# Gated MLP behind a gated linear attention: the gating multiply walks its columns in write order

## The chip, the cores and the metric

The kernel runs on one core of one Trainium2 chip. The metric is the device time of one execution in microseconds, the median of several runs. Five engines work side by side and meet through semaphores: TensorE (PE, with its weight loads PEld), VectorE (DVE), ScalarE (ACT), GpSimd (POOL) and SyncE (SP), which issues the transfers. Matmul results land in PSUM, eight banks of 512 float32 values per partition; everything else stays in SBUF.

## The reference, cut to what matters

A gated linear attention with 32 heads of width 48 over 768 tokens, and behind it a two-layer MLP whose activation is `h * cos(h)`:

```python
for t in range(S):
    state = f[:, :, t, :, None] * state + k[t] outer v[t]      # f = sigmoid(f_logit)
    y[:, :, t] = q[t] @ state
x = y as (4*768 tokens, 384)
h = x @ w_in            # 384 -> 2048
g = h * np.cos(h)       # the gating
out = g @ w_out         # 2048 -> 384
```

Inputs and output are float32; the kernel works in bfloat16 between them and accumulates in float32.

## The kernel before, in words

**Attention.** The tokens are taken in 12 pairs of 128-token chunks (`pair(n)`). For each pair the kernel loads f, k, q and v, forms decays on ACT and PE, decayed q and k on POOL, their transposes, the scores `sc` on PE, the masked scores `am` on DVE (L461), the carried state `st` and `sz` on DVE (L497, L503), and the outputs `y` and `yi` on PE. `xe` (DVE or ACT, L197) copies these into `x`, the MLP's input. A pair of chunks holds 256 tokens, of which each partition row loaded two neighbours; so inside a chunk of 128 columns the token order is e-major: column `64*e + n` holds token `2*n + e`.

**MLP.** `moe(m, t0, T)` takes a unit of T = 128 (the first two) or 256 tokens. The 2048 hidden features are computed in steps of 1024 columns of PSUM, which is two banks: step `h{m}.{j}` (PE, L579) is 4 feature blocks of 128 by 256 tokens (or 8 by 128), 12 matmuls of 256 columns (or 24 of 128). Step `co{m}.{j}` (ACT, L584) takes the cosine of these 1024 columns, as a sine with a phase, into the bfloat16 tile `co` in SBUF. Step `g{m}.{j}` (DVE, L561, function `gate`) multiplies `ph` (PSUM, float32) by `co` and writes `g` (SBUF, bfloat16). Steps `o{r}.{s}` (PE, L595) multiply four feature blocks of g with w_out, four matmuls of 384 columns each; `ot` copies the sums out of PSUM and `out` stores them.

**The token order in the gating.** `ph` and `co` have the e-major order of x. `g` is written in plain token order, column `2*n + e`, so that the output rows come out in order. So the multiply is also a permutation of each chunk's 128 columns, done by the access patterns of its three operands. There are 48 such multiplies, each over 128 partitions and 1024 columns.

**Order and buffers.** Every step has its engine and its place in one list written out by hand (`ORDER`). `g7.2:V` means that step g7.2 runs on DVE, and a number or letter behind it chooses engine and buffer; each engine runs its steps in this order. The PSUM tiles are four, of two banks each; an `h` step takes one whole tile (places T0, T2, T4, T6), and a tile is free for the next step when the gating that reads it has ended. Smaller results (scores, sums of `o`) use the same tiles. `co` has four buffers, `g` five.

Of the kernel before, what the change touches and what calls it, by code (L numbers as in the profile page):

```python
# [188 lines left out]
def describe(nc, cpool, ppool, q, k, v, f_logit, moe_w_in, moe_w_out, out):  # L189
# [368 lines left out]
    def gate(gv, ph, co, T):  # L558

        o = gv.ap if T == C else gv.ap.rearrange("p f (g t) -> p (f g) t", t=C)  # L560
        nc.vector.tensor_mul(out=o.rearrange("p b (n e) -> p b e n", e=2),  # L561
                             in0=ph.ap.rearrange("p (b e n) -> p b e n", e=2, n=64),
                             in1=co.ap.rearrange("p (b e n) -> p b e n", e=2, n=64))


    def moe(m, t0, T):
# [4 lines left out]
        for j in range(KF // F):  # L571
            ph, co = Val(p2), Val(coS)
            for s in range(2):
                def first(e, j=j, s=s, ph=ph):
                    xa = xw.ap if T == 2 * C else xw.ap[:, None]
                    for i in range(s * F // 2, (s + 1) * F // 2):
                        f0 = (j * F + i) * 128
                        for kk in range(KM):
                            nc.tensor.matmul(ph.ap[:, i * T:(i + 1) * T].rearrange("p (g t) -> p g t", t=C),  # L579
                                             lhsT=w_in_bf[:, kk, f0:f0 + 128], rhs=xa[:, :, kk, :], start=(i % (F // 2) == 0 and kk == 0),  # L580
                                             stop=((i + 1) % (F // 2) == 0 and kk == KM - 1))
                G.step(f"h{m}.{j}{s}", ("PE",), first, reads=[xw, w_in_v[(j * F + s * F // 2) // 4]],
                       writes=[ph], sums=True)
            G.step(f"co{m}.{j}", ("ACT",), lambda e, ph=ph, co=co: nc.scalar.activation(  # L584
                out=co.ap, in_=ph.ap, func=AF.Sin, bias=halfpi), reads=[ph], writes=[co], table="S")
            gv = gT.part(lambda a, j=j: a[:, j * F:(j + 1) * F, 0:T])
            G.step(f"g{m}.{j}", ("DVE",), lambda e, ph=ph, co=co, gv=gv: gate(gv, ph, co, T),
                   reads=[ph, co], writes=[gv])
# [129 lines left out]
```

## Time and profile before

| | |
|---|---|
| time, median of 3 runs | 183.58 us (183.56 to 183.68) |
| the profiled execution | 183.05 us, span 181.3 us |
| PE busy | 174.0 us, 96% of the span |
| DVE busy | 138.2 us, 76% |
| ACT busy | 130.7 us, 72% |
| POOL busy | 109.2 us, 60% |
| the gating, 48 instructions on DVE | 61.3 us busy, 1311 ns each |
| the cosine, 48 instructions on ACT | 52.7 us busy, 1113 ns each |

Busy times are those of one profiled execution; its time is 1.75 us longer than its span, which runs from the first to the last instruction. A group of instructions is named by source line, engine, operation and operands, with its count, busy time and the mean duration of one; behind a bar stands the idle time of the engine just before them and what ended it. Back-to-back instructions on DVE overlap a little in the records, so a group's busy time is less than count times mean.

### The profile page before, as it was taken

The page shows a single profiled execution, that of the slowest core. Times are in us where ns is not written, and L with a number is a line of the kernel's source. Part 1 is how long each engine was busy: PE and PEld are TensorE (multiplying, and loading weights), DVE is VectorE, ACT ScalarE, POOL GpSimd, SP SyncE. Part 2 cuts the span into 40 slices and gives each one's busy share as a digit, 9 for nine tenths or more (in the row PEclk, how much of TensorE's full clock was granted, in tenths as well). Part 3 has the DMA queues.
Part 4 walks back from the last instruction along what each step waited for, and adds up shares of the span by engine and source line. Part 5 has one row for each costly group of instructions (what it writes and reads, how often), then busy time and mean ns, then how long its engine had stood idle before and what let it go on. Part 6 is the DMA issues. An engine that isn't in the chain of part 4 may idle for free.

```text
span 181.3 us, 5818 instructions
## 1 busy us (share of the span) xinstructions
PE 174.0 (96%) x2464; PEld 124.2 (69%) x2464; DVE 138.2 (76%) x206; ACT 130.7 (72%) x187; POOL 109.2 (60%) x139
## 2 busy tenths in 40 slices
PE   7999788999999999999999999999999999999992
PEld 2555357785677876778657886658788767786661
DVE  5359988898685989897999698689888994466260
ACT  3985988778877999989997899769768452473221
POOL 4229889999969996989755968790799000000000
PEclk9999999999999999999999999999999999999999
DMA  6999999999999945996889999749929400110313
GB/s 141 261 261 263 346 304 318 293 283 281 317 264 241 270 77 128 253 230 133 125 162 317 189 242 253 175 125 244 216 85 197 90 4 0 38 52 4 130 43 130
DMA packets 72282, 33.93 MB, mean 187 GB/s; under 512 B 65344, under 2 KB 70720, under 8 KB 72256
## 3 DMA queue, kind: packets, MB, share of 16 engines
q1 hardware_dynamic: 71584, 33.27, 76.6%
q8 instruction: 19, 0.31, 0.7%
q10 hardware_dynamic: 672, 0.30, 0.6%
q14 instruction: 7, 0.06, 0.1%
HBM read 25.17 MB, written 4.72 MB: 165 GB/s over the span
## 4 chain that ended last, share of the span: by engine, by line
PE 80%; DMA 8%; SPq 5%; DVE 3%; POOL 1%; issue 1%; ACT 1%; POOLq 0%
PE ps L595 35%; PE ps L579 32%; DMA k<-in_k_dram 5%; PE ps L531 5%; SPq L296 3%; PE ps L456 3%; DMA v<-in_v_dram 3%; PE ps L479 2%; DVE g L561 1%; SPq L282 1%; PE ps L435 1%; PE ps L374 1%; DVE am L461 1%; POOL qk L404 1%; POOL k L351 1%
## 5 line engine op out<-in xcount | busy, mean ns | idle before, releaser
L561 DVE TENSOR_TENSOR g<-ps,co 128x1024 bf16<-128x1024 f32 x48 | 61.3, 1311 | 15.8 <-ACT co L584 14.8
L595 PE MATMUL ps<-w_out_bf,g 128*128 128x384 bf16 x384 | 68.9, 326 | 0.0
L579 PE MATMUL ps<-x,w_in_bf 128*128 128x256 bf16 (+1 forms) x624 | 68.2, 264 | 0.6 <-DVE x L197 0.5
L584 ACT ACTIVATE co<-ps,halfpi 128x1024 bf16<-128x1024 f32 x48 | 52.7, 1113 | 20.0 <-PE ps L579 19.8
L579 PEld LDWEIGHTS <-w_in_bf 128*128 128x128 bf16 x624 | 56.3, 98 | 9.3 <-DVE x L197 0.7
L595 PEld LDWEIGHTS <-g 128*128 128x128 bf16 x384 | 36.0, 98 | 21.5 <-issue 0.3
L461 DVE TENSOR_TENSOR am<-ps,pmask 128x1024 bf16<-128x1024 f32 x24 | 28.7, 1218 | 5.0 <-PE ps L456 4.8
L404 POOL TENSOR_TENSOR qk<-k,bi 128x384 bf16<-128x384 f32 x22 | 22.0, 1010 | 5.4 <-ACT bi L391 4.7
L404 POOL TENSOR_TENSOR qk<-q,b 128x384 bf16<-128x384 f32 x21 | 20.9, 1004 | 2.7 <-DVE q L338 2.1
L197 POOL COPY vt<-vb 64x384 bf16<-64x384 bf16 x33 | 16.7, 507 | 1.6
L264 PE MATMUL ps<-zero 128*128 128x512 bf16 x54 | 16.1, 426 | 1.2 <-DVE zero L203 1.2
L503 DVE TENSOR_TENSOR sz<-ps,b 64x192 bf16<-64x192 f32 x40 | 14.1, 353 | 2.5 <-PE ps L479 1.6
L341 POOL TENSOR_TENSOR q<-f,q 128x384 f32<-128x384 f32 x10 | 10.0, 1000 | 8.3 <-DMA q<-in_q_dram 6.1
L363 POOL TENSOR_TENSOR sp<-ls 128x384 bf16<-128x384 f32 x10 | 10.2, 1015 | 7.7 <-ACT ls L333 5.9
L329 ACT ACTIVATE f<-f 128x768 f32<-128x768 f32 (+1 forms) x14 | 10.4, 746 | 4.5 <-DMA f<-in_f_logit_dram 4.4
L351 POOL TENSOR_TENSOR k<-k,f 128x384 f32<-128x384 f32 (+1 forms) x12 | 11.1, 930 | 4.2 <-DMA k<-in_k_dram 4.2
L497 DVE TENSOR_TENSOR ps<-ps,sz 64x192 f32<-64x192 f32 x32 | 11.7, 366 | 1.9 <-PE ps L479 0.8
L197 ACT COPY ot<-ps 128x384 f32<-128x384 f32 (+1 forms) x14 | 6.1, 453 | 8.7 <-PE ps L595 8.7
L197 ACT CAST x<-ps 128x384 bf16<-128x384 f32 x12 | 5.5, 479 | 5.9 <-PE ps L531 5.9
L456 PE MATMUL ps<-qkt 48*64 48x128 bf16 (+1 forms) x304 | 8.7, 219 | 1.0 <-DVE sz L503 0.8
L197 DVE CAST x<-ps 128x384 bf16<-128x384 f32 x12 | 6.4, 552 | 4.0 <-PE ps L531 3.8
L264 PEld LDWEIGHTS <-zero 128*128 128x128 bf16 x54 | 4.9, 105 | 6.1 <-issue 2.2
(64 smaller groups left out, 167.5 us busy)
## 6 DMA issues: line engine op xcount, KB each, us to landing
v<-in_v_dram SPq DMA_DIRECT2D x12, 384.0 KB, 6.0
out_dram<-ot SPq DMA_DIRECT2D x22, 192.0 KB, 2.1
f<-in_f_logit_dram SPq DMA_DIRECT2D x10, 384.0 KB, 6.0
k<-in_k_dram SPq DMA_DIRECT2D x10, 384.0 KB, 6.7
q<-in_q_dram SPq DMA_DIRECT2D x10, 384.0 KB, 6.7
g<-in_moe_w_in_dram SPq DMA_DIRECT2D x4, 768.0 KB, 7.6
g<-in_moe_w_out_dram SPq DMA_DIRECT2D x4, 768.0 KB, 5.8
k<-in_k_dram SPq DMA_DIRECT2D x4, 192.0 KB, 4.5
```

The source lines that it names most:

```text
L197: (nc.scalar.copy if e == "ACT" else eng(e).tensor_copy)(out=o, in_=i)
L264: G.step(f"zf{i}", ("PE",), lambda e, dump=dump: nc.tensor.matmul(dump.ap, lhsT=zero[:, 0:128], rhs=zero, start=True, stop=True), writes=[ ...
L351: eng(e).tensor_mul(out=w.ap[:, :, 0, :], in0=w.ap[:, :, 0, :], in1=t.ap[:, :, 0, :])
L404: G.step(f"{nm}{n}.{u}", ("POOL", "DVE") if cut else ("POOL",), lambda e, u=u, j=j, src=src, dec=dec: eng(e).tensor_mul(out=qkp[u][j].ap[: ...
L456: nc.tensor.matmul(o[t0:t1, r, 2 * a + g, :].rearrange("p (e n) -> p e n", e=2), lhsT=wide[s, t0 // 64, :] if turned else wide[s].rearrang ...
L461: G.step(f"am{n}.{u}", ("DVE",), lambda e, u=u, sc=sc: nc.vector.tensor_mul(out=am[u].ap.rearrange("p r b n -> p (r b) n"), in0=sc.ap.rear ...
L497: nc.vector.tensor_add(out=view()[s], in0=view()[s], in1=S0.ap[s, :, r, :])
L503: eng(e).tensor_mul(out=new.ap[s, :, r, :].rearrange("p (u a) n -> p u a n", u=2), in0=view()[s].rearrange("p (u a) n -> p u a n", u=2), i ...
L561: nc.vector.tensor_mul(out=o.rearrange("p b (n e) -> p b e n", e=2), in0=ph.ap.rearrange("p (b e n) -> p b e n", e=2, n=64), in1=co.ap.rea ...
L579: nc.tensor.matmul(ph.ap[:, i * T:(i + 1) * T].rearrange("p (g t) -> p g t", t=C), lhsT=w_in_bf[:, kk, f0:f0 + 128], rhs=xa[:, :, kk, :], ...
L584: G.step(f"co{m}.{j}", ("ACT",), lambda e, ph=ph, co=co: nc.scalar.activation(out=co.ap, in_=ph.ap, func=AF.Sin, bias=halfpi), reads=[ph], ...
L595: nc.tensor.matmul(po.ap[:, 0:DM], lhsT=gT.ap[:, j, i * C:(i + 1) * C], rhs=w_out_bf[:, j, :], start=(po.first and j == 4 * s), stop=(po.f ...
```

## The change

In `gate` the names in the access patterns change place, from `p b e n` to `p b n e`, on all three operands:

```diff
     def gate(gv, ph, co, T):
         o = gv.ap if T == C else gv.ap.rearrange("p f (g t) -> p (f g) t", t=C)
-        nc.vector.tensor_mul(out=o.rearrange("p b (n e) -> p b e n", e=2),
-                             in0=ph.ap.rearrange("p (b e n) -> p b e n", e=2, n=64),
-                             in1=co.ap.rearrange("p (b e n) -> p b e n", e=2, n=64))
+        nc.vector.tensor_mul(out=o.rearrange("p b (n e) -> p b n e", e=2),
+                             in0=ph.ap.rearrange("p (b e n) -> p b n e", e=2, n=64),
+                             in1=co.ap.rearrange("p (b e n) -> p b n e", e=2, n=64))
```

The same products land in the same places. Before, the instruction walked along its inputs, column 0, 1, 2 and so on, and its writes went in steps of two bfloat16 elements (4 bytes), first the even and then the odd columns of a chunk. After, it walks along its output, column by column, and its reads alternate between the two halves of a chunk: 0, 64, 1, 65, 2, 66 and so on. In `ph` a step of 64 is 256 bytes of PSUM, in `co` it is 128 bytes of SBUF. Instruction count, engines, order, buffers and semaphores are those of before.

## The prediction

> **What bounds the kernel now.** I read the page first: the busy shares, then the chain of work that ended last.
>
> ```profile
> span 181.3 us, 5818 instructions
> PE 174.0 (96%) x2464; PEld 124.2 (69%) x2464; DVE 138.2 (76%) x206; ACT 130.7 (72%) x187; POOL 109.2 (60%) x139
> PE 80%; DMA 8%; SPq 5%; DVE 3%; POOL 1%; issue 1%; ACT 1%; POOLq 0%
> ```
>
> PE sets the time: it holds 80% of the chain, and the rest of it is the start (loads and their issue) and the last copies. DVE stands second with 138.2 of 181.3 us, and holds 3% of the chain. A dearer instruction on DVE therefore costs nothing until it makes PE wait. The waits of PE on DVE, all of them, are these:
>
> ```profile
> PE ps L264 <- DVE zero L203: 1.2, 1, 1.2
> PE ps L435 <- DVE qk L404: 1.0, 2, 0.8
> PE ps L456 <- DVE sz L503: 0.8, 1, 0.8
> PE ps L579 <- DVE x L197: 0.5, 1, 0.5
> PE ps L456 <- DVE qkt L197: 0.2, 1, 0.2
> ```
>
> 3.7 us in all, and none of it behind the gating. So the gating is late for nobody today. How much later it may get is a question of the stretches where it runs in a row. I take the five dense ones, then the whole middle and the end. The columns are the window, its length, and busy time and count by engine; an instruction that reaches over an edge is counted by its share. The second answer is the same for the gating line alone.
>
> ```profile
> 28.10:43.60 15.50, 14.65 (x218) 11.74 (x216) 14.65 (x15) 12.03 (x13) 15.27 (x15) 1.00 1.07 304
> 58.85:68.60 9.75, 9.75 (x119) 7.91 (x117) 9.23 (x8) 9.01 (x9) 8.78 (x11) 1.00 0.78 176
> 79.08:90.60 11.52, 11.52 (x172) 9.04 (x169) 10.42 (x12) 10.76 (x14) 10.43 (x12) 1.00 0.76 147
> 101.78:115.10 13.32, 13.32 (x167) 10.50 (x164) 10.17 (x9) 11.91 (x13) 10.27 (x12) 1.00 1.12 230
> 127.31:147.40 20.09, 20.09 (x287) 15.59 (x288) 17.87 (x19) 13.96 (x18) 11.98 (x16) 1.00 0.59 128
> 28.10:150.00 121.90, 121.05 (x1907) 90.72 (x1906) 105.25 (x141) 99.04 (x131) 92.27 (x111) 1.00 0.87 203
> 150.00:181.30 31.30, 28.01 (x253) 19.68 (x250) 13.90 (x15) 10.58 (x13) 0.00 (x0) 0.99 0.16 58
> ...
> 28.10:43.60 15.50, 10.20 (x8) 1.00 1.07 304
> ...
> 28.10:150.00 121.90, 51.10 (x40) 1.00 0.87 203
> 150.00:181.30 31.30, 10.21 (x8) 0.99 0.16 58
> ```
>
> From 28.10 to 150 us DVE (the third busy number) is at work for 105.25 of 121.90 us and runs 40 of the 48 gatings; in the five dense stretches it is at work for 14.65 + 9.23 + 10.42 + 10.17 + 17.87 = 62.34 of 70.18 us. The share of 76% over the whole span hides this: where the gating runs, DVE has 7.84 us left, and in the whole middle 16.65 us. Behind 150 us more than half of its time is free.
>
> **The change: the price of one gating.** Nothing is added, removed or moved; 48 instructions get other access patterns. Their price comes from three rows of groups on DVE:
>
> ```profile
> L561 DVE TENSOR_TENSOR g<-ps,co 128x1024 bf16<-128x1024 f32 x48 | 61.3, 1311 | 15.8 <-ACT co L584 14.8 <-POOL qk L404 0.6
> L461 DVE TENSOR_TENSOR am<-ps,pmask 128x1024 bf16<-128x1024 f32 x24 | 28.7, 1218 | 5.0 <-PE ps L456 4.8
> L197 DVE COPY ot<-ps 128x384 f32<-128x384 f32 x10 | 5.2, 550 | 0.9 <-PE ps L595 0.8
> ```
>
> The masked scores `am` are the same operation as the gating, from PSUM and SBUF to SBUF, on the same types and the same 1024 columns, but with all three operands read and written in runs of 128 and more. From `am` (1024 columns) and `ot` (384 columns), both out of PSUM, one column costs (1218 - 550) / 640 = 1.044 ns, and an instruction has 1218 - 1069 = 149 ns beside its columns. The gating is 93 ns above `am`. I read these 93 ns as the price of its stepped write, since `am` lacks nothing else that is plain to see; it is 0.09 ns a column, for one stream whose step is as small as it can be.
>
> No row shows DVE reading in steps of more than one element, so the new price is bounded from both sides. Below: the write becomes a plain run and the reads cost nothing, 1218 ns as `am`, 93 ns less than today. [...] I take 1931 ns, two thirds of the way up (1218 + 1069 x 2/3), 620 ns more than today. [...]
>
> [...]
>
> **From the price to the time.** 40 gatings in the middle add 40 x 0.62 = 24.8 us to DVE. At most, all of DVE's 16.65 idle us there take it up, and 8.2 us are left over; at least, only the idle time inside the dense stretches does, and 17.0 us are left. PE has no idle time there (121.05 of 121.90 us), so what makes PE wait is paid in full, and where PE waits, ACT's cosines and DVE's own next inputs come later too. To choose between the two I follow the fourth stretch:
>
> ```profile
> 100.56 9.33 PE L579 MATMUL ps<-x,w_in_bf 128*128 128x256 bf16 x84
> 103.87 5.03 DVE L561 TENSOR_TENSOR g<-ps,co 128x1024 bf16<-128x1024 f32 x4 [0.77 <-ACT co L584]
> 109.73 4.71 PE L595 MATMUL ps<-w_out_bf,g 128*128 128x384 bf16 x28
> 109.77 3.82 DVE L561 TENSOR_TENSOR g<-ps,co 128x1024 bf16<-128x1024 f32 x3 [0.87 <-ACT co L584]
> 115.10 1.23 DVE L461 TENSOR_TENSOR am<-ps,pmask 128x1024 bf16<-128x1024 f32 x1 [1.51 <-PE ps L456]
> ```
>
> 84 matmuls are seven steps h of 9.33 / 7 = 1.33 us. The last of them, h7.0, begins at about 108.56 and writes the tile that g8.2 leaves. g8.2 is the third of the row of four, which starts every (5.03 - 1.31) / 3 = 1.24 us, so it ends at 103.87 + 2.48 + 1.31 = 107.66: 0.9 us of cover. Three dearer gatings (the one before the row falls into the 0.77 us of idle time) put it 3 x 0.62 = 1.86 us later: PE stands 0.96 us. The next PE step, o11.3, takes the tile of g7.2, the fourth, which ends at 103.87 + 5.03 = 108.90 and then 4 x 0.62 = 2.48 later at 111.38; PE would come at 109.89 + 0.96 = 110.85: 0.53 us more, 1.5 us in all. DVE then runs its next three at 1.24 + 0.62 = 1.86 us, is done at about 111.38 + 3 x 1.86 = 116.96, and begins `am` at once, 1.86 us later than the 115.10 of today. The rule "added time less the idle time in the stretch" gives 8 x 0.62 - (13.32 - 10.17) = 1.8 us. So here the 17.0 rule holds, and most of it is seen by PE on the spot through the tiles that come free late. In the first stretch the rule is too strict, as an attention part with idle time follows it. I take 14.5 us, nearer to the upper end.
>
> Behind 150 us eight gatings come singly or by twos and threes with idle time ahead of them. The last one counts:
>
> ```profile
> 172.00 6.01 PE L595 MATMUL ps<-w_out_bf,g 128*128 128x384 bf16 x36
> 173.34 1.31 DVE L561 TENSOR_TENSOR g<-ps,co 128x1024 bf16<-128x1024 f32 x1 [3.25 <-ACT co L584]
> ```
>
> It is g12.0 and ends at 174.65. The 36 matmuls are nine steps o of 0.67 us, and the written order puts five of them ahead of o22.0, the first that reads it: 172.00 + 5 x 0.67 = 175.3. The cover is 0.7 us, and the added 0.62 us costs nothing there (0.3 us at the upper price).
>
> Sum, against the profiled execution's own 183.05 us (span 181.3 and 1.75 around it): 183.05 + 14.5 = 197.6 us. The median of the runs, 183.58, is 0.53 above that execution, so the forecast is **198 us**. With the price's upper end the middle adds 39.0 us, of which 22.4 to 31.2 remain: up to 215 us. A price of 1600 ns adds 11.6 us, of which 3.8 remain by the stricter rule: 187 us. The forecast's own range is 187 to 215.
>
> **The rivals.** *The reads cost nothing.* Each read stream alternates between two places, and each of the two advances one element at a time; if the engine keeps both neighbourhoods at hand, it pays nothing for that, and the write is plain as for `am`. The gating then takes 1218 ns, 93 less. For it: nothing in the profile, which has no such read; against it: the 93 ns themselves, a price for a milder walk. As PE waits nowhere for the gating, the gain is confined to the place where the chain runs through it. Of the chain in order of time these are the pieces:
>
> ```profile
> 28.10 1.33 DVE g L561
> ...
> 30.64 1.23 DVE g L561
> ```
>
> Two gatings, 2 x 0.093 = 0.2 us: 183.4 us, not slower. This case decides if the gating's row stays below some 1310 ns. [...]
>
> *The hops add.* PSUM and SBUF may each ask a cycle of its own, three in all: 149 + 3 x 1069 = 3356 ns, 2.05 us more; the middle adds 82 us, of which 65 to 74 remain, about 250 us. Anything above 2287 ns belongs here, from 215 us on. [...]
>
> *The cover is enough.* With a price between 1310 and 1600 ns the 40 gatings add less than 12 us, and the idle time of the middle takes up most of it: 183.6 to 187 us. For it: PE waits nowhere for the gating today. Against it: the dense stretches leave DVE 7.84 us for 40 gatings, 0.2 us each.
>
> That the multiply is carried out in the old order all the same, as the two orders give the same result, would leave 1311 ns and 183.6 us; I know no row that speaks for it.
>
> **How the numbers follow.** The measurement can tell about 0.2%, 0.37 us, from no change. Chances: the forecast (1600 to 2287 ns) 0.65, free reads 0.15, the hops add 0.10, the cover 0.08, the old order 0.02. Slower takes the forecast, the adding hops and 0.06 of the cover: 0.81. Free reads split into 0.07 faster and 0.08 the same, as 0.2 us lies inside what can be told; with 0.02 of the cover and 0.02 of the old order the same has 0.12. The range of 8 in 10 takes in the free reads at 183.2 and ends at the forecast's upper end of 215.
>
> **What would show it.** The gating's group should read near 1930 ns x48 (about 93 us) and DVE near 168 us. PE should lose its gapless stretches at L579 and L595, with new waits on "DVE g L561", and DVE should go over 90% between 28 us and the end of the attention; ACT's cosine should keep 1113 ns. If the gating reads near 1930 ns but the time is under 192 us, the step from DVE to PE was wrong; if the gating reads below 1600 or above 2287 ns, the price was.

## The result, and the profile after

The changed kernel takes 182.91 us (median of 21 runs, 182.29 to 183.44) against 183.41 us of the kernel before (21 runs): the ratio is 0.9972, with a 95% interval of 0.9959 to 0.9985. Measured once more beside other kernels it was 0.9983 (0.9964 to 1.0003). The first interval excludes a ratio of 1, the second just contains it. So it is a little faster, by 0.3 to 0.5 us, where 198 us was forecast. The median lies 0.3 us below the range's lower end of 183.2.

The page of the kernel after, busy shares and chain:

```profile
span 180.9 us, 5814 instructions
PE 172.6 (95%) x2460; PEld 123.9 (69%) x2464; DVE 134.6 (74%) x206; ACT 130.7 (72%) x187; POOL 109.2 (60%) x139
PE 81%; DMA 7%; ACT 3%; DVE 3%; SPq 2%; issue 1%; ACTq 0%
```

DVE has 3.6 us less to do; the chain is PE's as before. The groups of the gating and of the masked scores show why:

```profile
L561 DVE TENSOR_TENSOR g<-ps,co 128x1024 bf16<-128x1024 f32 x48 | 57.4, 1220 | 18.0 <-ACT co L584 16.7
L461 DVE TENSOR_TENSOR am<-ps,pmask 128x1024 bf16<-128x1024 f32 x24 | 28.7, 1218 | 5.2 <-PE ps L456 4.9
```

The gating costs 1220 ns, as the masked scores do: the surcharge of 93 ns is gone and the alternating reads cost nothing that can be told (2 ns). Of the 3.9 us that the gating's busy time loses (61.3 to 57.4), 2.2 us turn up as idle time ahead of it (15.8 to 18.0). The window of the whole middle says the same: DVE at 101.91 instead of 105.25 us, PE at 121.23 instead of 121.05 of 121.90 us.

```profile
28.10:150.00 121.90, 121.23 (x1909) 91.04 (x1904) 101.91 (x141) 99.01 (x131) 91.60 (x110) 1.00 0.85 201
```

What reached the end can be followed in the order of time. First the kernel before, from the first gating to the second pause for attention; then the kernel after:

```profile
28.10 1.33 DVE L561 TENSOR_TENSOR g<-ps,co 128x1024 bf16<-128x1024 f32 x1 [0.65 <-POOL qk L404]
...
37.93 5.14 DVE L561 TENSOR_TENSOR g<-ps,co 128x1024 bf16<-128x1024 f32 x4
39.75 0.82 PE L579 MATMUL ps<-x,w_in_bf 128*128 128x256 bf16 x6
40.57 0.45 PEld L595 LDWEIGHTS <-g 128*128 128x128 bf16 x4 [0.28 <-issue]
40.60 0.81 PE L595 MATMUL ps<-w_out_bf,g 128*128 128x384 bf16 x4
...
44.07 1.47 PE L595 MATMUL ps<-w_out_bf,g 128*128 128x384 bf16 x8
```

```profile
27.95 1.23 DVE L561 TENSOR_TENSOR g<-ps,co 128x1024 bf16<-128x1024 f32 x1 [0.65 <-issue]
...
37.64 3.48 DVE L561 TENSOR_TENSOR g<-ps,co 128x1024 bf16<-128x1024 f32 x3
39.45 0.82 PE L579 MATMUL ps<-x,w_in_bf 128*128 128x256 bf16 x6
40.11 0.45 PEld L595 LDWEIGHTS <-g 128*128 128x128 bf16 x4
40.14 0.81 PE L595 MATMUL ps<-w_out_bf,g 128*128 128x384 bf16 x4
...
43.61 1.47 PE L595 MATMUL ps<-w_out_bf,g 128*128 128x384 bf16 x8
```

Counted from the first gating, PE's h step at 39.75 comes 11.65 us later before and 11.50 after (-0.15), and the first o step 12.50 and 12.19 (-0.31). The second difference is a wait that the table of waits does not list. This first o step is o2.0, and in the written order it takes the PSUM tile T0, which g0.1, the second gating of the row at 37.93, has to read first. Before, g0.1 starts at 39.15 and ends at 40.45. PE's weight loads for o2.0 begin 0.12 us later, at 40.57, after 0.28 us of standing idle, although the six matmuls ahead, which start 0.109 us apart, 0.66 us in all, would by an estimate from that have let PE go on at 40.41. After, g0.1 ends at 39.99 and the loads begin at 40.11, again 0.12 us later; PE is ready just then (39.45 + 0.66). The eight-matmul o step then stands at 15.97 and 15.66 us. From there to the last row of 36 o matmuls it is 172.00 - 44.07 = 127.93 before and 171.58 - 43.61 = 127.97 after: no further gain is seen in the following 128 us. A gain of a few tenths would not be seen here, since the changed kernel, profiled a second time, took 172.00 - 43.61 = 128.39 us for this stretch.

### The profile page after: what moved, and what is told of

It is laid out like the page before. It is cut to its first block, busy times and chain, and to the rows that moved or that the text cites. A ratio compares the mean times of both kernels' runs of the same rounds, so it can differ in the third digit from the quotient of the medians.

```text
span 180.9 us, 5814 instructions
## 1 busy us (share of the span) xinstructions
PE 172.6 (95%) x2460; PEld 123.9 (69%) x2464; DVE 134.6 (74%) x206; ACT 130.7 (72%) x187; POOL 109.2 (60%) x139
## 4 chain that ended last, share of the span: by engine, by line
PE 81%; DMA 7%; ACT 3%; DVE 3%; SPq 2%; issue 1%; ACTq 0%
PE ps L595 35%; PE ps L579 33%; PE ps L531 5%; DMA f<-in_f_logit_dram 4%; PE ps L456 4%; DMA v<-in_v_dram 3%; SPq L296 2%; PE ps L479 2%; DVE g L561 1%; PE ps L435 1%; PE ps L374 1%; DVE am L461 1%; PE ps L264 1%; ACT f L344 0%; ACT f L329 0%
## 5 line engine op out<-in xcount | busy, mean ns | idle before, releaser
L561 DVE TENSOR_TENSOR g<-ps,co 128x1024 bf16<-128x1024 f32 x48 | 57.4, 1220 | 18.0 <-ACT co L584 16.7
L584 ACT ACTIVATE co<-ps,halfpi 128x1024 bf16<-128x1024 f32 x48 | 52.7, 1113 | 19.8 <-PE ps L579 19.5
L461 DVE TENSOR_TENSOR am<-ps,pmask 128x1024 bf16<-128x1024 f32 x24 | 28.7, 1218 | 5.2 <-PE ps L456 4.9
L264 PE MATMUL ps<-zero 128*128 128x512 bf16 x50 | 14.6, 412 | 1.5 <-DVE zero L203 1.2
```

Source lines behind the costliest of these rows:

```text
L264: G.step(f"zf{i}", ("PE",), lambda e, dump=dump: nc.tensor.matmul(dump.ap, lhsT=zero[:, 0:128], rhs=zero, start=True, stop=True), writes=[ ...
L461: G.step(f"am{n}.{u}", ("DVE",), lambda e, u=u, sc=sc: nc.vector.tensor_mul(out=am[u].ap.rearrange("p r b n -> p (r b) n"), in0=sc.ap.rear ...
L561: nc.vector.tensor_mul(out=o.rearrange("p b (n e) -> p b n e", e=2), in0=ph.ap.rearrange("p (b e n) -> p b n e", e=2, n=64), in1=co.ap.rea ...
```

## The experiments

The first question is where the time came from; the second what a read or a write in steps costs; the third whether the prediction's rule from price to time holds.

**The new order in the first eight gatings alone (early), and in the other 40 alone (late).** The edit, shortened:

```diff
+        if m <= 2:          # early; late: m > 2
             nc.vector.tensor_mul(out=o.rearrange("p b (n e) -> p b n e", e=2), ...)
+        else:
+            nc.vector.tensor_mul(out=o.rearrange("p b (n e) -> p b e n", e=2), ...)
```

Expected of early:

> The new order only in the eight gatings of units 0 to 2 (the first 43 us), the old order in the other 40. Theory: PE waits nowhere for the gating except through the start of its chain, so the whole gain comes from the first gatings and this kernel keeps it: ratio to before near 0.997, eight gatings at 1220 ns, forty at 1311. Rival: each of the 48 gatings gives its share of the gain; then eight of 48 give a ratio near 0.9995, which is the same as before.

Expected of late:

> The new order only in the 40 gatings of units 3 to 12, the old order in the first eight. Theory: PE is covered there, so 40 x 0.09 = 3.6 us less on DVE turn into idle time of DVE and the ratio is 1.000 (0.999 to 1.001). Rival (equal shares): 0.9977.

Measured: early 183.47 against 183.62 us, ratio 0.9989 (0.9978 to 0.9999); late 183.49 us, ratio 0.9999 (0.9989 to 1.0009). Their groups, early first, show that both did what they say:

```profile
L566 DVE TENSOR_TENSOR g<-ps,co 128x1024 bf16<-128x1024 f32 x40 | 51.1, 1309 | 15.0 <-ACT co L589 14.7
L562 DVE TENSOR_TENSOR g<-ps,co 128x1024 bf16<-128x1024 f32 x8 | 9.6, 1217 | 1.0 <-POOL qk L404 0.7 <-ACT co L589 0.3
```

```profile
L562 DVE TENSOR_TENSOR g<-ps,co 128x1024 bf16<-128x1024 f32 x40 | 47.8, 1220 | 17.1 <-ACT co L589 16.3
L566 DVE TENSOR_TENSOR g<-ps,co 128x1024 bf16<-128x1024 f32 x8 | 10.2, 1315 | 0.7 <-issue 0.7
```

Late has 3.3 us less gating and no gain. Its interval rules out equal shares of all 48 gatings, which would have given 0.9977; early's own interval does not rule them out (0.9995). In early's order of time the same o step as above comes 43.55 - 27.90 = 15.65 us behind the first gating, in late's 44.06 - 28.09 = 15.97: the 0.31 us are the first eight gatings'. That is a ratio of 0.9983, inside the intervals of early and of the changed kernel. The 0.997 expected of early was too much. Whether the other 40 add one or two tenths of a microsecond the runs cannot tell.

**The changed kernel again (after2).**

> The changed kernel once more, beside the kernel before and on the same chip as the other three. If 0.3 us of gain from the first eight gatings is all there is, the ratio is 0.998 to 0.9985; if the other 40 add to it, 0.997 or below.

0.9983 (0.9964 to 1.0003), 183.14 against 183.60 us. It fits 0.3 us, but its interval does not exclude the other case, and the two medians lie 0.46 us apart.

**Reads in other walks (read_a).** The 44 gatings of units 2 to 12 in four kinds, each on its own line; s is 2, 8 or 32. This kernel and the next three on reads and writes were run once each, so a price below is that of 8 to 11 instructions in one run:

```diff
+            nc.vector.tensor_mul(out=flat.rearrange("p (s a) -> p s a", s=8),
+                                 in0=ph.ap.rearrange("p (a s) -> p s a", s=8),
+                                 in1=co.ap.rearrange("p (a s) -> p s a", s=8))
```

> The 44 gatings of units 2 to 12 write a plain run and read both inputs in other walks, eleven each: plain; every second column, twice over; every eighth column, eight times over (128 places visited in turn); every 32nd (32 places in turn). The order of g's columns is left wrong by this. Theory A (reads never pay for a step): all four 1218 to 1225 ns. Theory B (the engine keeps only a few neighbourhoods at hand, two in the changed kernel): plain and every second column near 1220, every eighth and every 32nd column dearer, up to 2290 ns. If plain reads and a plain write come out below 1218 ns, something in the changed gating still pays.

The groups: L568 plain, L572 every second column, L576 every eighth, L580 every 32nd.

```profile
L576 DVE TENSOR_TENSOR g<-ps,co 128x1024 bf16<-128x1024 f32 x11 | 21.9, 2004 | 0.9 <-ACT co L603 0.8
L580 DVE TENSOR_TENSOR g<-ps,co 128x1024 bf16<-128x1024 f32 x11 | 20.8, 1898 | 3.6 <-ACT co L603 3.6
...
L572 DVE TENSOR_TENSOR g<-ps,co 128x1024 bf16<-128x1024 f32 x11 | 13.4, 1221 | 3.3 <-ACT co L603 3.0
L568 DVE TENSOR_TENSOR g<-ps,co 128x1024 bf16<-128x1024 f32 x11 | 13.4, 1218 | 4.8 <-ACT co L603 4.7
```

So reads in steps can cost what was forecast, 1.9 to 2.0 us, but not every such read does: theory A falls.

**Which memory, and how many places (read_b).** The same with 512, 256 and 128 columns between places, and steps of 32 on one input alone.

> As the first run on reads, eight or nine gatings each: two places in turn, 512 columns apart (for PSUM in different banks); four places, 256 apart; eight places, 128 apart; 32 places in steps of 32 from PSUM alone with co read plainly; the same from co alone with PSUM read plainly (the order of g's columns is left wrong by this). Theory (a few neighbourhoods are kept at hand): two places 1220 ns whatever their distance; a jump to some 1900 ns at four or at eight places tells how many are kept. For the source: if each memory charges alike and the two overlap, both single ones read near 1900 ns; if only SBUF or only PSUM charges, one reads 1220. Rival (it is the length of the step that costs, not the number of places): two places at 512 dearer than 1220.

L568 is two places, L572 four, L576 eight, L580 steps of 32 from PSUM alone, L584 steps of 32 from SBUF alone.

```profile
L568 DVE TENSOR_TENSOR g<-ps,co x9: 1208/1220/1234, 38.3 to 175.4; 128x1024 bf16<-128x1024 f32 x9
L572 DVE TENSOR_TENSOR g<-ps,co x9: 1917/1932/1951, 42.1 to 169.3; 128x1024 bf16<-128x1024 f32 x9
L576 DVE TENSOR_TENSOR g<-ps,co x8: 1912/1943/1960, 59.2 to 164.3; 128x1024 bf16<-128x1024 f32 x8
L580 DVE TENSOR_TENSOR g<-ps,co x9: 1214/1223/1225, 34.2 to 180.1; 128x1024 bf16<-128x1024 f32 x9
L584 DVE TENSOR_TENSOR g<-ps,co x9: 1870/1891/1925, 35.4 to 172.3; 128x1024 bf16<-128x1024 f32 x9
```

The columns behind the count are minimum, median and maximum in ns. In steps of 32 columns the PSUM read costs nothing that can be told (L580, 128 bytes, 1223 ns); all of the price is the SBUF read's (L584, 64 bytes, 1891 ns). Two places are free at both distances run, 64 columns (1220 ns in the changed kernel) and 512 (1220 ns); four, 256 apart, are not (1932 ns), and three were not run. Steps of 32 are the only walk that was run on each memory alone.

**Two places or near neighbours (read_c).** Walks that tell "two places are kept" from "a neighbour was read just before" (the line of `co` of each; `ph` is read in the same walk, `out` written plainly):

```diff
+  in1=co.ap.rearrange("p (a s) -> p s a", s=4)               # every fourth
+  in1=co.ap.rearrange("p (a s e) -> p e s a", a=2, e=2)      # two places, each by 2
+  in1=co.ap.rearrange("p (a s e) -> p e s a", a=2, e=8)      # two places, each by 8
+  in1=co.ap.rearrange("p (a s r) -> p s a r", a=4, r=2)      # four places, runs of 2
+  in1=co.ap.rearrange("p (a s r) -> p s a r", a=4, r=4)      # four places, runs of 4
```

> [...] Walks: every fourth column (8 bytes of co); two places 512 columns apart, each moving on by 2 columns (4 bytes, so that no 4-byte word is visited twice); the same, each moving on by 8 columns (16 bytes); four places with runs of 2 columns (4 bytes); four places with runs of 4 columns (8 bytes). Theory P (two places are kept at hand): both two-place walks 1220 ns, four places about 1940 with runs of 2 and of 4 alike or less with runs. Theory N (an element is cheap when it lies near one read one or two elements before, whatever the number of places): two places moving on by 2 near 1220, moving on by 8 near 1940 or above, as the 2004 of every eighth column; runs of 4 in four places near 1220.

In that order, L568 to L584:

```profile
L568 DVE TENSOR_TENSOR g<-ps,co x9: 1211/1217/1226, 38.0 to 171.2; 128x1024 bf16<-128x1024 f32 x9
L572 DVE TENSOR_TENSOR g<-ps,co x9: 1215/1229/1240, 41.8 to 165.1; 128x1024 bf16<-128x1024 f32 x9
L576 DVE TENSOR_TENSOR g<-ps,co x8: 2069/2078/2089, 58.8 to 160.7; 128x1024 bf16<-128x1024 f32 x8
L580 DVE TENSOR_TENSOR g<-ps,co x9: 1216/1223/1225, 34.1 to 175.7; 128x1024 bf16<-128x1024 f32 x9
L584 DVE TENSOR_TENSOR g<-ps,co x9: 1206/1217/1225, 35.4 to 167.4; 128x1024 bf16<-128x1024 f32 x9
```

Theory P falls: two places are dear when each moves on by 16 bytes (2078 ns). The three forecasts of theory N came true, and the two other walks fit it: the walks over co that were free are those in which every read had another close to it, next to it in order or with one other read between. For neighbours in order 8 bytes were near enough (every fourth column, 1218 ns) and 16 were not (every eighth, 2004 ns); with one read between 4 bytes were (1229 ns) and 16 were not (2078 ns); distances between these were not run. The changed gating reads 0, 64, 1, 65 of each chunk (1220 ns), so the next read but one is 2 bytes on. That the price of the dear walks is SBUF's was shown for steps of 32 alone (L580 and L584 of read_b, 1223 and 1891 ns); in the others a price of PSUM could hide behind that of SBUF.

**Writes in other walks (write_a).** Both inputs read plainly, `out` in steps:

```diff
+            nc.vector.tensor_mul(out=flat.rearrange("p (a s) -> p s a", s=2),
+                                 in0=ph.ap.rearrange("p (s a) -> p s a", s=2),
+                                 in1=co.ap.rearrange("p (s a) -> p s a", s=2))
```

> The 44 gatings read both inputs plainly and write g in other walks, eight or nine each: two places in turn, 512 apart; every second column (the step of the old gating, over 1024 columns); every eighth; every 32nd; every 128th, eight places (the order of g's columns is left wrong by this). If the 93 ns of the old gating are the price of its stepped write, every second column reads near 1310 ns, and longer steps the same or more. Rival (the 93 ns came from something else in the old pattern, such as its 16 runs of 64): every second column near 1220 ns.

L568 two places, L572 every second column, L576 every eighth, L580 every 32nd, L584 every 128th:

```profile
L568 DVE TENSOR_TENSOR g<-ps,co x9: 4664/4714/4923, 44.2 to 280.3; 128x1024 bf16<-128x1024 f32 x9
L572 DVE TENSOR_TENSOR g<-ps,co x9: 1290/1311/1528, 52.4 to 268.6; 128x1024 bf16<-128x1024 f32 x9
L576 DVE TENSOR_TENSOR g<-ps,co x8: 4686/4742/4949, 69.7 to 258.1; 128x1024 bf16<-128x1024 f32 x8
L580 DVE TENSOR_TENSOR g<-ps,co x9: 4622/4834/4886, 34.0 to 287.7; 128x1024 bf16<-128x1024 f32 x9
L584 DVE TENSOR_TENSOR g<-ps,co x9: 4689/4914/4927, 38.3 to 274.2; 128x1024 bf16<-128x1024 f32 x9
```

Every second column has the old gating's 1311 ns, without its runs of 64: the 93 ns are the stepped write's. With each longer step run (16, 64 and 256 bytes) the instruction took a median of 4742 to 4914 ns, and with two places in turn 4714. This kernel took 300.25 us, with a granted TensorE clock of 0.84; the masked scores on DVE read 1231 ns in it, near their 1218, so DVE's rows can be compared. A walk that was free for reads, two places 512 columns apart (1220 ns in read_b), made the instruction almost four times as long in the write (4714 ns). Writes in steps of 8 bytes or in short runs were not tried.

**The forecast's price, in a kernel that has it (many).** All 44 gatings of units 2 to 12 read both inputs in steps of 32 and write a plain run.

> The 44 gatings of units 2 to 12 read both inputs in steps of 32 columns, 32 places in turn, and write a plain run (the order of g's columns is left wrong by this). Their price should be near 1900 ns, close to the 1931 ns of the forecast, so this run shows what the forecast's second step gives at the forecast's own price. 36 of them lie between 28 and 150 us: 36 x 0.59 = 21 us more on DVE. By the prediction's rule 4.5 to 13.4 us, about 11 where it was taken (ratio near 1.06). Rival, from the run with the additional multiply, which gave 29 us where the stricter end of the rule gave about the same: at or above the stricter end, 13 us or more (ratio 1.07 or more).

197.59 us against 183.60, ratio 1.0762 (1.0747 to 1.0778), with this group, these waits for the gating (the three longest) and this window:

```profile
L567 DVE TENSOR_TENSOR g<-ps,co 128x1024 bf16<-128x1024 f32 x44 | 81.2, 1891 | 8.9 <-ACT co L590 8.7
```

```profile
PE ps L585 <- DVE g L567: 5.2, 10, 0.9
PE ps L456 <- DVE g L567: 2.0, 4, 1.1
PE ps L601 <- DVE g L567: 1.3, 4, 0.4
```

```profile
28.10:150.00 121.90, 112.37 (x1709) 82.98 (x1707) 112.31 (x128) 93.34 (x122) 91.97 (x111) 1.00 0.84 198
```

36 of these gatings lie between 28 and 150 us and add 36 x (1.891 - 1.311) = 20.9 us; less the 7.84 us of the dense stretches the stricter rule gives 13.0, and 14.0 were measured. The 11 us that were expected came out too low, and the rival on record (13 us or more) came true. PE waits for the gating mainly at L585, the h steps, whose tiles come free late, as the prediction worked out for one stretch. PE has lost its gapless middle: 112.37 of 121.90 us.

**A dearer gating by another way (dear).** One more multiply ahead of each gating:

```diff
+        nc.vector.tensor_mul(out=spare, in0=co.ap[:, 0:512], in1=co.ap[:, 512:1024])
         nc.vector.tensor_mul(out=o.rearrange("p b (n e) -> p b e n", e=2), ...)
```

> The old gating with one more multiply on DVE ahead of each of the 48 (512 columns of co into a spare float32 tile), which waits for the same cosine: about 149 + 512 x 1.044 = 684 ns by its row, about 0.6 us net of overlap. It tries the second step of the prediction, from the price of a gating to the time, apart from the first. If the step was right: 0.6 us more on each gating give 8 to 17 us, near 14 (ratio about 1.07 to 1.08). Rival: the idle time of DVE and PE's cover take up most of it, under 6 us (ratio under 1.033).

The ratio is 1.1532 (1.1489 to 1.1576), 28 us more, far over the expectation; but the multiply itself was dearer than its estimate of 684 ns:

```profile
L562 DVE TENSOR_TENSOR spare<-co 128x512 f32<-128x512 bf16 x48 | 43.7, 909 | 9.5 <-ACT co L586 9.4
```

The first 40 multiplies, those of the middle, took 38.1 us together; less 7.84 the stricter rule gives 30.3 us, 2 us above the 28 measured. The mean of 909 ns hides two kinds: the 18 multiplies during which no POOL instruction ran took 665 to 693 ns, as estimated, and the other 30 took 672 to 1522 ns, 1048 on average. POOL was busy for 119.8 us instead of 109.2. So the multiply and POOL's instructions were longer where they ran side by side; no run takes this cause apart. It also makes dear the less clean of the two tests, as POOL's busy time rose with DVE's; in many POOL kept its 109.1 us.

## Why the prediction was wrong, point by point

**The bound: right.** PE sets the time before and after, DVE is second, and time taken from or given to DVE counts only where PE waits for it. Late shows the first half (3.3 us off, no gain), many and dear the second.

**The price of one gating: wrong, and this is the step that failed.** The lower end was right: 1218 ns came true with 1220, and the reading of the 93 ns as the stepped write's is shown by write_a. No run shows, for this walk, the 1931 ns that the sum uses, the author's estimate between 1218 ns and an upper end of 2287 ns, nor that upper end for any read: the changed gating took 1220 ns, the dearest read walk 2079 ns, and the prediction's own sign for a wrong price, a gating below 1600 ns, appeared. The prediction held the 93 ns against free reads, as the price of a milder walk, but this was a price of writing, and in these runs writes and reads differed: a gating with two places in turn took 1220 ns in the read and 4.7 us in the write. Nor did both streams charge in the walk where each was run alone, steps of 32 columns (PSUM 1221 ns, SBUF 1889 ns in the mean), and what told the free walks from the dear ones in SBUF was whether a place was read again right away (two places moving on by 4 bytes 1229 ns, by 16 bytes 2078). 1931 ns is near what a gating cost that read four, eight or 32 places in turn, a column at each (1889 to 1941 ns), which the change doesn't do.

**From price to time: right in kind, near the stricter end.** The rule "added time less the idle time of the dense stretches" gives 13.0 us for many and 30.3 for dear, where 14.0 and 28.1 were measured; the milder end (all idle time of the middle helps) gives 4.2 and 21.5. The 14.5 us that the prediction took between its ends of 8.2 and 17.0 were, by many, somewhat mild. That many's 197.59 us equals the forecast's 197.6 is a coincidence: many has 36 dear gatings in the middle and not 40.

**The end: nothing was seen there.** The last gating takes 1.23 instead of 1.31 us, PE's last row of 36 matmuls 6.01 us as before.

**The rivals.** "The reads cost nothing" is what happened; it had 0.15. Its reason, two neighbourhoods kept at hand, was nearly right; read_c puts the near neighbour in its place. Its gain was put at 0.2 us by two gatings on the chain; the first eight give 0.31, as PE also waited a little for the tile of the second gating of the row at 37.93. That wait was missing from the table of waits, on which "PE waits nowhere for the gating" rested: the records show PE as busy until 40.57 (39.75 + 0.82), although its six matmuls start 0.109 us apart. With 0.31 for 0.2 the case would have stood at 183.27 us against 183.58. Of the 0.36 us from there to 182.91, 0.17 is that the kernel before, too, came out lower, at 183.41 over 21 runs; the other 0.19 us lie inside the intervals, and where they come from stays open.

## What to carry to other kernels

Before pricing a stepped access on DVE, ask for each operand whether it is read or written and in which memory, and for a read from SBUF how near the next read, or the next but one, falls (here 8 bytes to the next were near enough, 1218 ns, and 16 were not, 2004 ns). In each of the five walks run both ways here the read was cheaper than the write (1220 to 2004 ns against 1311 to 4914), which speaks for a permutation on the read side, with the write left plain. The surcharge seen on one operand, 93 ns on the write, said nothing of the price on another (2 ns for the changed gating's reads); a kernel with each walk on a line of its own gives four or five such prices in one run. A second engine's slack is to be counted inside the stretches where its work is dense, not over the span. And where the order written out by hand shows a tile passing from one engine to the next, a wait of 0.2 us can be real, as here (40.41 to 40.57), although the table of waits does not list it.

## What the runs showed of the hardware that was not expected

DVE's bfloat16 writes to SBUF in steps: 0.09 ns a column above a plain run at 4 bytes, but (4714 - 149) / 1024 = 4.5 ns a column at two places in turn, and about the same for steps of 16, 64 and 256 bytes (4742, 4834 and 4914 ns). DVE's float32 reads from PSUM cost nothing that can be told over a plain read (1218 ns) in steps of 32 columns (1223), at every second (1221) and every fourth column (1218), and with two places in turn (1220); in the walks where SBUF was dear a price of PSUM's own cannot be told. In SBUF, runs of two bfloat16 elements, 4 bytes, in four places are already free (1223 ns). A multiply with both inputs in SBUF took 665 to 693 ns while POOL stood still and up to 1522 ns beside POOL's instructions.
